# A hand-written order for three engines in blocks 2 to 8 of an FNet and MLP kernel

## The chip, the cores and the metric

The kernel runs on one core of one Trainium2 chip. Its metric is the device time of one execution in microseconds. A core has TensorE for matrix products, ScalarE and VectorE for elementwise work, GpSimd (POOL in the profile) and SyncE (SP), which here issues loads. Each engine works through its own list of instructions in a fixed order; where an instruction needs another engine's result, it waits at its place, and all behind it on that engine wait too.

## The reference

`x` has 2048 rows of 576 numbers. Its rows are normalized, and two branches are added to it: a Fourier mixing and an MLP.

```
xn = (x - mean(x)) / sqrt(var(x) + 1e-5)                      # over the 576
a, b = xn @ dft_hid_re.T, xn @ dft_hid_im.T                   # 576 x 576
y = dft_seq_re @ a - dft_seq_im @ b                           # 2048 x 2048
out = x + y + relu(xn @ w1) @ w2                              # w1 576 x 4608, w2 4608 x 576
```

All inputs are float32. The kernel splits each operand of a product into a high and a low half in float16 and adds three products of halves.

## The kernel before

**The MLP.** The 4608 hidden columns are cut into nine blocks of 512 (`b`, 0 to 8), the 2048 rows into four groups of 512 (`g`, 0 to 3). One pair (b, g) is a step; step n = 4b + g. In blocks 2 to 8, steps 8 to 35, both products of a step are done by a scheme of Strassen and Winograd with seven products of half size.

`step_products(n)` gives the first layer of a step: products P1, P5, P6, P2, P7, P3, P4 (`product`, line 579), which accumulate in four banks of PSUM: `u`, `v` and `w`, the last one of two in turn. P1 leaves a sum in `u`, P6 and P7 add to it, and so on, so each bank has to be read at the right time: `c11`, `c22`, `r21` and `s4` are copies by ScalarE; the adds to `c11` (from `v`), `c22` (from `u`) and `r21` (from `w`) are VectorE's. From these come the operands of the second layer in float16, a high part by ScalarE and a low part by VectorE: for A11, A22 and A12 (`value`, `last`) and for the sums S1 to S4 (`end_hi`, `end_lo`, two halves each). `rests` (line 598) are eight small matmuls for the last 64 rows of the inner dimension, of this step's P3 and P4 and of the next step's P2 and P5.

`mlp2(b, g, n)` (line 685) is product n = 0 to 6 of the second layer, called m0 to m6 below: 12 matmuls into one of two accumulators of two banks each, and then its drain. For n = 0, 2, 3, 6 ScalarE copies the bank with a scale (line 710), for n = 1, 4, 5 VectorE adds it (line 714). After n = 1, 4, 5, 6 GpSimd issues a transfer that adds the result to a buffer in DRAM (`spill`, line 717). m0, m2, m4 and m6 go into one accumulator one after another, m3 and m5 into another, so the drain of one stands before the next. The second layer runs one step behind the first: within step n the m's are those of step n - 1.

**The order in a step** is the tuple at lines 1197 to 1204. It is the order in which the program names its instructions:

```
(run, P1), (left, 0), (run, P5), (end, 0), (end, 0), (m, 0), (brief, 1), (left, 1),
(run, P6), (end, 0), (end, 0), (run, P2), (t_sum, 0), (m, 1), (used, P2), (more, 0), (ready, 1),
(run, P7), (t_sum, 0), (ready, 1), (m, 2), (used, P7), (count, 0), (m, 3), (brief, 1),
(rest, 0), (run, P3), (brief, 1), (m, 4), (used, P3), (t_sum, 0), (ready, 1),
(run, P4), (used, P4), (t_sum, 0), (m, 5), (ready, 1), (count, 0),
(m, 6), (brief, 3),
```

The framework's planner makes each engine's list from it. It takes the named order as a priority and lets a later instruction go ahead where it reckons that an earlier one isn't ready. `tc.issue_after(i)` makes an instruction stand behind instruction i on its engine; `behind(key)` (line 243) does so with an instruction kept in `order`.

**Preparing the next block.** In the four steps of block b the weights of block b + 1 are loaded and made ready. `prepare_block` (line 876) lists this as 39 small steps in `todo`; `work()` (line 1037) takes the next one, and `brief` and `ready` in the tuple call it ten times in a step. In that list: loads of two halves of W1 (`load_w1`, SyncE); their largest magnitudes (`max_w1`, VectorE), a reduction over the partitions on GpSimd, a power of two from it (`power`, tiny instructions on VectorE); the split into halves (`split_w1b`, ScalarE and then VectorE, line 229 and 230); the sums of quarters that the scheme needs (`sums_w1`, lines 774 to 778); the same for W2 (`sum_w2` on ScalarE, `split_w2`, `sums_w2`). In block 8 the list has the hidden DFT matrix instead (`power_d`, `prepare_d`, `load_d`; line 1092 and 1096).

**Counts.** Beside that, the magnitudes of the sequence DFT matrices are summed, 64 blocks of 512 KB, one after another through one buffer. `part(k)` (line 1153) takes the block that has been loaded (`sum_c`, line 1145, ScalarE) and starts the load of the next (line 1138, SyncE). Six parts of the hidden DFT matrix (`first_d` and `max_d`, a maximum on VectorE) stand in the same list at places 24 to 29. A step calls `count` twice, and `more` a third time where g is odd. Three parts are taken before step 8, ten in each later block.

**After the steps** comes the product with the hidden DFT matrix (line 1324), whose first pass also has the second layer of the last step, in an order that is already fixed for TensorE, ScalarE and VectorE by `pinned` (line 1442); then the product with the sequence DFT matrices (line 1570).

Of the kernel before, what the change touches and what calls it, by code (L numbers as in the profile page):

```python
# [26 lines left out]
NQ = NF // 2  # L27
# [27 lines left out]
def kernel(  # L55
# [496 lines left out]
    banks1, ends, gates = [], [], {}  # L552
# [6 lines left out]
    def step_products(n):  # L559
# [57 lines left out]
        def value(q, src):  # L617
            hi, lo = h[:, 0, q], h[:, 1, q]
            nc.scalar.activation(hi, src, AF.Relu)  # L619
            stt(lo, src, 0.0, hi, ALU.max, ALU.subtract)  # L620

        def end_hi(i):
            with behind("free"):
                order["s"] = nc.scalar.activation(h[:, 0, S1 + 2 * i :][:, :2], stage[:, 1 + 2 * i :][:, :2], AF.Copy).ins  # L624
# [5 lines left out]
        def sums_h():  # L630
            nc.scalar.activation(r21, r21, AF.Relu)
            stt(s3, c11, 0.0, r21, ALU.max, ALU.subtract)
            stt(s1, c22, 0.0, r21, ALU.max, ALU.add)
            stt(s2, c22, 0.0, s3, ALU.max, ALU.subtract)

        def last():
            hi, lo = h[:, 0, A12], h[:, 1, A12]
            nc.scalar.activation(hi, s4, AF.Copy)
            tt(lo, s4, hi, ALU.subtract)
            tt(s4, s4, s2, ALU.subtract)  # L640
            for i in range(NQ):
                ends.extend((lambda i=i: end_hi(i), lambda i=i: end_lo(i)))

        free = {
            P1: lambda: freed(nc.scalar.activation(c11, u, AF.Copy)),
            P2: lambda: freed(tt(c11, v, c11, ALU.add), "vfree"),
            P6: lambda: freed(nc.scalar.activation(r21, u, AF.Copy)),  # L647
            P5: lambda: freed(nc.scalar.activation(c22, w, AF.Copy)),
            P7: lambda: freed(tt(c22, u, c22, ALU.add), "vfree"),  # L649
            P3: lambda: freed(tt(r21, w, r21, ALU.add), "vfree"),  # L650
            P4: lambda: freed(nc.scalar.activation(s4, u, AF.Relu)),
        }
        use = {
            P2: lambda: value(A11, c11),
            P7: lambda: value(A22, c22),
            P3: sums_h,
            P4: last,
        }
# [26 lines left out]
    def mlp2(b, g, n):  # L685

# [8 lines left out]
        for c in range(2):  # L695
            for i in range(NQ):
                h, w = hs[b, g, i], w2s[b, i]
                for j, (x, y) in enumerate(((0, 0), (0, 1), (1, 0))):
# [4 lines left out]
                    ).ins  # L703
        if n in (0, 2, 3, 6):
# [325 lines left out]

    steps = [(b, g) for b in range(NB) for g in range(NG)]
# [89 lines left out]

    NP = NT // 2
# [28 lines left out]
    parts[24:24] = [(first_d, max_d, m) for m in range(ND)]  # L1151
# [13 lines left out]
    for n in range(2, len(steps)):  # L1165
        b, g = steps[n]
        pb, pg = steps[n - 1]
        if g == 0 and b:
            if b + 1 < NB:
                todo += prepare_block(b + 1)  # L1170
            else:
                d = power_d()
                todo += [lambda: (load_d(0), next(d)), lambda: None, lambda: later(d)]
                todo += prepare_d(0) + [lambda: load_d(1)] + [lambda: None] * 3 + prepare_d(1)[:DA]
# [10 lines left out]
        if b >= BB:  # L1185
            run, rests = step_products(n)
            used = lambda q: run(q, True)
            m = lambda q: mlp2(pb, pg, q)
            end = lambda q: ends and ends.pop(0)()
            ready = lambda q: [work() for _ in range(q)]  # L1190
            brief = lambda q: [work(True) for _ in range(q)]
            count = lambda q: passes and passes.pop(0)()
            left = lambda q: n == 2 * NG and lates[-1][q]()
# [74 lines left out]
    while todo:  # L1268
        work()
# [371 lines left out]
```

## Time and profile before

| | |
|---|---|
| median of 3 runs | 1233.02 us (1230.89 to 1233.25) |
| profiled execution | 1233.9 us, span 1232.1 us |
| granted clock of TensorE, mean over the span | 0.999 |
| steps 8 to 35 | from 194 to 792 us of the span |
| busy: TensorE, VectorE, ScalarE, GpSimd | 98%, 81%, 57%, 15% |

How to read it. A row of instruction groups has the line, the engine, the operation, what it writes and reads, the number of instructions, then busy time and the mean of one, and then the idle time of the engine before them with what ended it. PE is TensorE, PEld its loading of weights, DVE is VectorE, ACT is ScalarE. In a timeline the first two columns are the start and the duration in us; a part in brackets is idle time of that engine just before and what ended it. In the chain of work that ended last, the columns are start, duration and what. A row of waits has the total, the number and the longest.

Matmuls overlap: 26 matmuls of the steps start within 2.84 us, though each is listed with 0.27 us. So the busy share of TensorE says little, and the spacing of its starts is what counts. Some records of matmuls are missing from a trace.

### The profile page before, as it was taken

The page shows a single profiled execution, that of the slowest core. Times are in us where ns is not written, and L with a number is a line of the kernel's source. Part 1 is how long each engine was busy: PE and PEld are TensorE (multiplying, and loading weights), DVE is VectorE, ACT ScalarE, POOL GpSimd, SP SyncE. Part 2 cuts the span into 40 slices and gives each one's busy share as a digit, 9 for nine tenths or more (in the row PEclk, how much of TensorE's full clock was granted, in tenths as well). Part 3 has the DMA queues.
Part 4 walks back from the last instruction along what each step waited for, and adds up shares of the span by engine and source line. Part 5 has one row for each costly group of instructions (what it writes and reads, how often), then busy time and mean ns, then how long its engine had stood idle before and what let it go on. Part 6 is the DMA issues. An engine that isn't in the chain of part 4 may idle for free.

```text
span 1232.1 us, 24558 instructions
## 1 busy us (share of the span) xinstructions
PE 1211.8 (98%) x10173; PEld 957.2 (78%) x10173; DVE 999.3 (81%) x1629; ACT 707.8 (57%) x1073; POOL 189.6 (15%) x229
## 2 busy tenths in 40 slices
PE   8999999999999999999999999999999999999998
PEld 7665557888888788888888877877777777777776
DVE  8998899778887887778877877567898878787875
ACT  5756456776675576767767766555654333333332
POOL 2431211112121111112121211234300000000000
PEclk9999999999999999999999999999999999999999
DMA  8994545767566666667576666620165244433320
GB/s 314 209 155 106 76 74 139 149 143 156 125 155 141 144 152 162 138 161 155 132 157 142 147 151 149 106 35 1 62 194 162 94 155 161 153 122 131 128 88 20
DMA packets 84063, 164.64 MB, mean 134 GB/s; under 512 B 22640, under 2 KB 43632, under 8 KB 83952
## 3 DMA queue, kind: packets, MB, share of 16 engines
q1 hardware_dynamic: 61168, 120.61, 30.8%
q0 software_dynamic: 22784, 42.48, 24.0%
q8 instruction: 79, 1.29, 0.4%
q14 instruction: 32, 0.26, 0.1%
HBM read 110.76 MB, written 53.08 MB: 133 GB/s over the span
## 4 chain that ended last, share of the span: by engine, by line
PE 66%; DVE 18%; issue 7%; ACT 4%; DMA 4%; POOL 1%; SPq 0%; ACTq 0%; POOLq 0%; DVEq 0%
PE p L1570 24%; PE p L699 19%; PE bank L593 16%; DVE arena L230 3%; PE U L1324 3%; PE W L1324 2%; DMA arena<-in_w_dram 1%; PE p L392 1%; DVE arena L714 1%; DMA spill<-arena 1%; DVE arena L468 1%; ACT arena L229 1%; PE bank L612 1%; DVE c_mf L161 1%; DVE arena L628 1%
## 5 line engine op out<-in xcount | busy, mean ns | idle before, releaser
L699 PE MATMUL p<-arena 128*128 128x288 f16 x3024 | 400.5, 286 | 8.4 <-DVE arena L714 6.6
L699 PEld LDWEIGHTS <-arena 128*128 128x128 f16 x3024 | 295.7, 98 | 86.3 <-issue 10.3
L1570 PE MATMUL p<-arena 128*128 128x288 f16 x2688 | 329.9, 286 | 0.4 <-DVE arena L1576 0.4
L1570 PEld LDWEIGHTS <-arena 128*128 128x128 f16 x2688 | 263.0, 98 | 67.1 <-issue 0.7
L593 PE MATMUL bank<-arena 128*128 128x256 f16 x2580 | 304.8, 273 | 1.3 <-ACT arena L647 0.9
L593 PEld LDWEIGHTS <-arena 128*128 128x128 f16 x2580 | 250.1, 98 | 39.3 <-issue 7.7
L229 ACT ACTIVATE arena<-arena,sc_c 128x1024 f16<-128x1024 f32 x112 | 124.3, 1144 | 194.3 <-DVE arena L1422 69.7
L717 POOL DMA_DIRECT2D spill<-arena x144 | 128.6, 914 | 568.3 <-DVE arena L714 520.4
L230 DVE SCALAR_TENSOR_TENSOR arena<-arena,sc_c 128x1024 f16<-128x1024 f32 x112 | 140.9, 1281 | 47.7 <-ACT arena L229 47.7
L710 ACT ACTIVATE arena<-p,c_ub 128x576 f32<-128x576 f32 x144 | 105.5, 734 | 44.2 <-PE p L699 40.6
L230 DVE SCALAR_TENSOR_TENSOR arena<-arena,c_sw 128x640 f16<-128x640 f32 (+2 forms) x118 | 98.2, 847 | 20.2 <-ACT arena L229 19.8
L229 ACT ACTIVATE arena<-arena,c_sw 128x640 f16<-128x640 f32 (+3 forms) x118 | 90.1, 795 | 23.4 <-DVE c_sw L171 12.2
L628 DVE TENSOR_TENSOR arena<-arena 128x1024 f16<-128x1024 f32 x56 | 68.5, 1223 | 42.3 <-ACT arena L624 42.1
L392 PE MATMUL p<-arena 128*128 128x128 f16 (+1 forms) x680 | 100.0, 304 | 1.2 <-ACT arena L347 1.1
L714 DVE SCALAR_TENSOR_TENSOR arena<-p,c_ub,arena 128x576 f32<-128x576 f32 x108 | 87.4, 810 | 8.4 <-PE p L699 5.6
L1324 PEld LDWEIGHTS <-arena 128*128 128x128 f16 x738 | 71.6, 98 | 19.7 <-issue 1.9
L392 PEld LDWEIGHTS <-arena 128*128 128x128 f16 x680 | 53.9, 100 | 39.6 <-issue 3.8
L619 ACT ACTIVATE arena<-arena 128x512 f16<-128x512 f32 x56 | 35.2, 628 | 66.4 <-DVE arena L649 37.9
L1145 ACT ACTIVATE arena<-arena 128x1024 f32<-128x1024 f32 x64 | 67.0, 1048 | 6.4 <-DMA arena<-in_cim_dram 3.4
L1576 DVE SCALAR_TENSOR_TENSOR arena<-p,us_c,arena 128x288 f32<-128x288 f32 x112 | 57.5, 513 | 13.8 <-PE p L1570 13.4
L624 ACT ACTIVATE arena<-arena 128x1024 f16<-128x1024 f32 x56 | 58.8, 1050 | 0.0
L1324 PE MATMUL U<-arena 128*128 128x288 f16 x400 | 55.8, 286 | 0.0
(151 smaller groups left out, 1098.6 us busy)
## 6 DMA issues: line engine op xcount, KB each, us to landing
spill<-arena POOLq DMA_DIRECT2D x144, 288.0 KB, 4.8
arena<-in_cre_dram SPq DMA_DIRECT2D x64, 512.0 KB, 4.0
arena<-in_cim_dram SPq DMA_DIRECT2D x64, 512.0 KB, 4.8
arena<-in_w_dram SPq DMA_DIRECT2D x17, 640.0 KB, 5.9
arena<-in_w_dram SPq DMA_DIRECT2D x18, 576.0 KB, 4.7
arena<-spill SPq DMA_DIRECT2D x40, 144.0 KB, 2.2
arena<-in_x_dram SPq DMA_DIRECT2D x16, 288.0 KB, 7.1
spill<-in_x_dram SPq DMA_DIRECT2D x16, 288.0 KB, 6.2
```

The costliest lines, as they stand in the source:

```text
L229: nc.scalar.activation(hi, src, AF.Copy, scale=s).ins,
L230: nc.vector.scalar_tensor_tensor(lo, src, s, hi, ALU.mult, ALU.subtract).ins,
L392: order["m1"] = nc.tensor.matmul(ps[:, cols], w1s[b, i // 2][:, hl, i % 2 * KT + k], xT[g][:, kx, cols], start=(start and n == 0), stop=(s ...
L593: nc.tensor.matmul(ps[:, i], l, r, start=first and i == m == 0, stop=m == len(todo) - 1, skip_group_check=not first or i > 0,)
L628: order["lo"] = nc.vector.tensor_tensor(lo, stage[:, 1 + 2 * i :][:, :2], hi, ALU.subtract).ins
L699: order["pe"] = nc.tensor.matmul(ps[:, c], h[:, x, qa, c * P : (c + 1) * P], w[:, y, qb], start=first and i == 0 and j == 0, stop=i == NQ ...
L710: freed(nc.scalar.activation(o, ps, AF.Copy, scale=us[b]))
L714: add = nc.vector.scalar_tensor_tensor(o, ps, us[b], o, ALU.mult, ALU.add)
L717: nc.gpsimd.dma_start(spill[g, row, col], o, accum_op=ALU.add)
L1145: nc.scalar.activation(f, f, AF.Abs, scale=2.0**-10, accum_out=sums_c[:, n, q : q + 1])
L1324: nc.tensor.matmul(ps, l, r, start=first and m == 0, stop=m == len(todo) - 1, skip_group_check=not first,)
L1570: nc.tensor.matmul(ps, w[:, a, k], r[:, c, RQ[rq]], start=first and k == 0 and j == 0, stop=k == HK - 1 and j == 2, skip_group_check=not f ...
```

## The change

From step 8 on every piece of work in a step goes through `pinned`, which has moved up in the file: it makes each instruction that a piece puts on TensorE, ScalarE or VectorE stand behind the last instruction that an earlier piece put on that engine. The planner then has nothing to choose on these three engines. SyncE and GpSimd aren't pinned.

The order of TensorE's products in the tuple stays P1, P5, m0, P6, P2, m1, P7, m2, m3, `rests`, P3, m4, P4, m5, m6. The copies, adds, high and low parts are now named one by one. `mlp2` is cut into its matmuls (`mlp2_mm`) and its drain with the spill (`mlp2_out`); the drain of m6, `s42` (the last of the sums), `lo0`, `hi1` and `lo1` are done in the next step, as `pend`.

The preparation of the next block no longer comes from a list that is worked off; `chores_w(b)`, or `chores_d()` in block 8, gives each piece a step g and a slot, a to g, of the tuple. What is left of the preparation of this block's W2, three splits, stands in slot b of step g = 0, with the loads of the next W1 behind it.

`max_d` goes from places 24 to 29 of the counts to places 11, 21, 31, 41, 51 and 61, one in each block from 2 to 7. The counts of a step stand behind P2, behind the drain of m3 where g is odd, and behind `hi0`.

```diff
-        def run(q, used=False):
-            if used:
-                return use[q]()
-            product(q)
-            if q in free:
-                free[q]()
-
-        return run, rests
+        ops = {q: (lambda q=q: product(q)) for q in (P1, P2, P3, P4, P5, P6, P7)}
+        ops.update({
+            "c11": copy(c11, u), "v": add(c11, v), "r21": copy(r21, u), "c22": copy(c22, w),
+            "u": add(c22, u), "w": add(r21, w), "s4": copy(s4, u, AF.Relu),
+            "hi11": hi(A11, c11), "lo11": lo(A11, c11), "hi22": hi(A22, c22), "lo22": lo(A22, c22),
+            "relu": lambda: nc.scalar.activation(r21, r21, AF.Relu),
+            "s3": lambda: stt(s3, c11, 0.0, r21, ALU.max, ALU.subtract),
+            "s1": lambda: stt(s1, c22, 0.0, r21, ALU.max, ALU.add),
+            "s2": lambda: stt(s2, c22, 0.0, s3, ALU.max, ALU.subtract),
+            "hi12": hi(A12, s4, AF.Copy),
+            "lo12": lambda: tt(h[:, 1, A12], s4, h[:, 0, A12], ALU.subtract),
+            "s42": lambda: tt(s4, s4, s2, ALU.subtract),
+        })
...
+    def pinned(f, *a):
+        traced = nc.cur_bb.bb.instructions
+        n = len(traced)
+        with ExitStack() as s:
+            for i in tails.values():
+                s.enter_context(tc.issue_after(i))
+            f(*a)
+        for i in traced[n:]:
+            if i.engine in ENGINES:
+                tails[i.engine] = i
...
+    def chores_w(b):
+        c, n = {}, b + 1
+        c[0, "b"] = todo[:] or [lambda i=i, k=k: split_w2(b, i, k) for i, k in ((0, 2), (1, 1), (1, 2))]
+        del todo[:]
+        c[0, "b"] += [lambda i=i: load_w1(n, i) for i in range(NQ)]
+        for i in range(NQ):
+            p = power_w1(n, i)
+            c[i, "e"] = [lambda i=i: max_w1(n, 2 * i)]
+            c[i, "f"] = [lambda i=i, p=p: (max_w1(n, 2 * i + 1), next(p))]
+            c[i + 1, "a"] = [lambda p=p: next(p, None)]
+            c[i + 1, "b"] = [lambda i=i, k=k: split_w1b(n, i, k) for k in (0, 1)]
+            c[i + 1, "c"] = [lambda i=i: sums_w1(n, i)]
+            c[i + 1, "d"] = [lambda i=i, k=k: split_w1b(n, i, k) for k in (2, 3)] + [lambda i=i: load_w2(n, i)]
+        p2 = power_w2(n)
+        c[2, "e"] = [lambda: sum_w2(n, 0)]
+        c[2, "g"] = [lambda: (sum_w2(n, 1), next(p2))]
+        c[3, "a"] = [lambda: next(p2, None)]
+        c[3, "b"] = [lambda: split_w2(n, 0, 0)]
+        c[3, "c"] = [lambda: sums_w2(n, 0)]
+        c[3, "d"] = [lambda: split_w2(n, 1, 0)]
+        c[3, "e"] = [lambda: sums_w2(n, 1)]
+        c[3, "f"] = [lambda: split_w2(n, 0, 1)]
+        return c
+
+    def chores_d():
+        c, d = {}, power_d()
+        c[0, "b"] = [lambda i=i, k=k: split_w2(NB - 1, i, k) for i, k in ((0, 2), (1, 1), (1, 2))] + [lambda: load_d(0)]
+        c[0, "e"] = [lambda: next(d)]
+        c[1, "a"] = [lambda: next(d, None)]
+        e0, e1 = prepare_d(0), prepare_d(1)
+        for k, q in zip("bcdef", (e0[:2], e0[2:4], e0[4:6], e0[6:7], e0[7:8])):
+            c[1, k] = q
+        c[2, "b"] = e0[8:] + [lambda: load_d(1)]
+        c[2, "f"] = e1[:1]
+        for k, q in zip("bcd", (e1[1:3], e1[3:4], e1[4:5])):
+            c[3, k] = q
+        return c
...
-    parts[24:24] = [(first_d, max_d, m) for m in range(ND)]
+    for m in range(ND):
+        parts.insert(11 + 10 * m, (first_d, max_d, m))
...
+            if n == BB * NG:
+                pend = {"lo0": lates[-1][0], "hi1": lates[-1][1]}
+            ops, rests = step_products(n)
+            now = lambda k: pinned(ops[k])
+            then = lambda k: pinned(pend.pop(k)) if k in pend else None
+            m = lambda q: pinned(mlp2_mm, pb, pg, q)
+            out2 = lambda q: pinned(mlp2_out, pb, pg, q)
+            slot = lambda k: [pinned(f) for f in chores.pop((g, k), ())]
...
-                (run, P1), (left, 0), (run, P5), (end, 0), (end, 0), (m, 0), (brief, 1), (left, 1),
...
-                (m, 6), (brief, 3),
+                (now, P1), (then, "out6"), (then, "s42"), (now, "c11"), (slot, "a"), (then, "lo0"),
+                (now, P5), (slot, "b"), (now, "c22"), (then, "hi1"),
+                (m, 0), (slot, "c"), (out2, 0), (now, P6), (now, "r21"), (slot, "d"),
+                (now, P2), (count, 0), (now, "v"), (now, "hi11"), (m, 1), (out2, 1),
+                (now, P7), (now, "u"), (now, "lo11"), (now, "hi22"), (m, 2), (out2, 2), (then, "lo1"), (slot, "e"),
+                (m, 3), (out2, 3), (slot, "f"), (more, 0), (t_sum, 0), (rest, 0), (now, P3), (now, "w"), (now, "relu"), (t_sum, 0), (now, "lo22"),
+                (slot, "g"), (m, 4), (out2, 4), (now, "s3"), (now, "s1"), (now, "s2"),
+                (now, P4), (now, "s4"), (now, "hi12"), (now, "hi0"), (t_sum, 0), (count, 0), (m, 5), (out2, 5), (now, "lo12"),
+                (t_sum, 0), (m, 6),
             ):
                 do(q)
+            pend = {k: ops[k] for k in ("s42", "hi1", "lo0", "lo1")}
+            pend["out6"] = lambda b=pb, g=pg: mlp2_out(b, g, 6)
...
-                (P1, 0), ("end", 0), ("end", 0), ("c11", 0), ("mlp", 0), ("end", 0), ("end", 0),
+                (P1, 0), ("pend", "out6"), ("pend", "s42"), ("c11", 0), ("pend", "hi1"), ("pend", "lo0"),
+                 ("mlp", 0), ("pend", "lo1"),
```

More of the change, by code (lines that the diff above doesn't have):

```diff
@@ L1167 @@
         pb, pg = steps[n - 1]
[L1168 to L1174, printed above, removed]
+        if g == 0 and 0 < b < BB:
+            todo += prepare_block(b + 1)
+        if g == 0 and b >= BB:
+            chores = chores_w(b) if b + 1 < NB else chores_d()
         if b == 0 and g + 1 < NG:
@@ L1185 @@
         if b >= BB:
[L1186 to L1193, printed above, removed]
-            t_sum = lambda q: next(tq, None)
+            if n == BB * NG:
+                pend = {"lo0": lates[-1][0], "hi1": lates[-1][1]}
@@ L1197 @@
+            rest = lambda q: pinned(rests, n + 1 if n + 1 < len(steps) else None)
             for do, q in (
[L1198 to L1201 removed]
```

79 lines of the change are left out of this document (25 added, 54 removed).

## The prediction

> **What bounds the kernel now.** I read the page first, for the engines' shares, then the chain of work that ended last, then the timeline of TensorE, then the waits of TensorE alone from 188 to 800 us, where the steps lie that the change touches.
>
> ```profile
> span 1232.1 us, 24558 instructions
> PE 1211.8 (98%) x10173; PEld 957.2 (78%) x10173; DVE 999.3 (81%) x1629; ACT 707.8 (57%) x1073; POOL 189.6 (15%) x229
> ...
> 210.22 1.64 PE bank L593 x14
> 231.21 1.63 PE bank L593 x14
> ...
> 784.17 1.63 PE bank L593 x14
> ```
>
> The last three rows, of the chain, are the start of product P3 in the first, the second and the last of the 28 steps. A step without a stall lasts 231.21 - 210.22 = 20.99 us (its neighbours give 20.98). From the first P3 to the last are 27 steps: 784.17 - 210.22 = 573.95 us, where 27 x 20.98 would be 566.46. So only 7.5 us of stall lie in 27 steps. The first step is counted apart, with the calendar of a quiet step (timeline of TensorE):
>
> ```profile
> 194.17 3.22 PE L593 MATMUL bank<-arena 128*128 128x256 f16 x28
> ...
> 210.16 1.70 PE L593 MATMUL bank<-arena 128*128 128x256 f16 x14
> ...
> 217.63 3.00 PE L593 MATMUL bank<-arena 128*128 128x256 f16 x26
> 220.47 1.63 PE L699 MATMUL p<-arena 128*128 128x288 f16 x12
> 221.94 3.00 PE L593 MATMUL bank<-arena 128*128 128x256 f16 x26
> 224.78 1.63 PE L699 MATMUL p<-arena 128*128 128x288 f16 x12
> 226.25 1.47 PE L593 MATMUL bank<-arena 128*128 128x256 f16 x12
> 227.56 3.10 PE L699 MATMUL p<-arena 128*128 128x288 f16 x24
> 230.60 0.61 PE L612 MATMUL bank<-arena 64*128 64x256 f16 x8
> 231.14 1.70 PE L593 MATMUL bank<-arena 128*128 128x256 f16 x14
> 232.68 1.63 PE L699 MATMUL p<-arena 128*128 128x288 f16 x12
> ```
>
> From P1 to P3 the first step takes 210.16 - 194.17 = 15.99 us, the quiet one 231.14 - 217.63 = 13.51. The first has four matmuls more (28 and 28 for 26 and 26), at (220.47 - 217.63) / 26 = 0.109 us each, so it loses 2.04. Ceiling of any gain in the steps: 7.5 + 2.0 = 9.5 us, 0.8%. Who holds TensorE:
>
> ```profile
> PE p L699 <- DVE arena L714: 3.9, 5, 2.1
> PE bank L612 <- DVE arena L649: 1.2, 1, 1.2
> PE bank L593 <- ACT arena L647: 0.9, 1, 0.9
> PE p L699 <- DVE arena L628: 0.6, 1, 0.6
> PE bank L593 <- ACT arena L645: 0.2, 1, 0.2
> ...
> 417.63 1.47 PE L593 MATMUL bank<-arena 128*128 128x256 f16 x12 [0.94 <-ACT arena L647]
> ...
> 739.51 1.63 PE L699 MATMUL p<-arena 128*128 128x288 f16 x12 [2.09 <-DVE arena L714]
> ...
> 734.01 0.82 DVE L230 SCALAR_TENSOR_TENSOR arena<-arena,c_sd 128x576 f16<-128x576 f32 x1 [3.68 <-DMA spill<-arena]
> ...
> L161 DVE TENSOR_REDUCE max_d<-arena x6: 1144/1145/1153, 397.6 to 441.5; 128x1 f32<-128x960 f32 x6
> ```
>
> These waits add to 6.8 us; the rest of the 9.5 hides under the modelled ends of the matmuls before. Most wait for VectorE, which drains a bank (L714) or frees one (L649) too late. Two places explain themselves: six `max_d` of 1.145 us each fall into block 4 (397.6 to 441.5), and in block 8 a split stands in VectorE's queue for 3.68 us, until the spill of an old buffer has landed, before the drain that TensorE needs.
>
> **The change part by part.** *TensorE.* Its order P1, P5, m0, P6, P2, m1, P7, m2, m3, rests, P3, m4, P4, m5, m6 is the one that the rows show; pinning it is worth nothing, and no matmul goes. The work of ScalarE, VectorE and the queues is the same but for places. So the change is worth the stalls it takes away less those it makes.
>
> *The steady step.* I lay the new order of the fullest kind (g = 1: two scale steps, both splits, sums, three counts) against the calendar, P1 at 0: m0 2.84, P6 4.31, m1 7.15, P7 8.62, m2 9.93, m3 11.40, rests 12.97, P3 13.51, m4 15.05, P4 16.52, m5 18.05, m6 19.52, next step 20.99. Durations:
>
> ```profile
> L628 DVE TENSOR_TENSOR arena<-arena 128x1024 f16<-128x1024 f32 x56 | 68.5, 1223 | 42.3 <-ACT arena L624 42.1
> L714 DVE SCALAR_TENSOR_TENSOR arena<-p,c_ub,arena 128x576 f32<-128x576 f32 x108 | 87.4, 810 | 8.4 <-PE p L699 5.6
> 232.88 0.69 DVE L650 TENSOR_TENSOR arena<-bank,arena 128x512 f32<-128x512 f32 x1 [0.39 <-PE bank L593]
> L230 DVE SCALAR_TENSOR_TENSOR arena<-arena,c_sw 128x640 f16<-128x640 f32 (+2 forms) x118 | 98.2, 847 | 20.2 <-ACT arena L229 19.8
> L624 ACT ACTIVATE arena<-arena 128x1024 f16<-128x1024 f32 x56 | 58.8, 1050 | 0.0
> L710 ACT ACTIVATE arena<-p,c_ub 128x576 f32<-128x576 f32 x144 | 105.5, 734 | 44.2 <-PE p L699 40.6
> L619 ACT ACTIVATE arena<-arena 128x512 f16<-128x512 f32 x56 | 35.2, 628 | 66.4 <-DVE arena L649 37.9
> 230.77 1.04 ACT L1145 ACTIVATE arena<-arena 128x1024 f32<-128x1024 f32 x1
> 231.71 0.19 ACT L1145 ACTIVATION_READ_ACCUMULATOR arena<-arena 128x1 f32 x1
> ```
>
> A bank is readable 0.2 us after its product (232.88 against 231.14 + 14 x 0.109). ScalarE: the drain of m6 before to 0.9, `c11` 1.5 to 2.1, two splits to 3.3, `c22` 3.8, `hi1` 4.8, drain of m0 5.4, `r21` 5.8 to 6.4 (P7 asks at 8.62), two splits to 7.8, a count to 8.85. VectorE: `s42`, scales and `lo0` to 2.4, splits to 4.3, five sums to 6.3, splits 7.2 to 8.8, `v` 8.7 to 9.4 although P2 was readable at 7.35, drain of m1 to 10.1 (m3 asks at 11.40: slack 1.3, the least), `u` 10.1 to 10.8 (rests 12.97), `lo11`, `lo1` to 12.6 (m4 15.05), two maxima to 14.3, `w` 15.2 to 15.9, drain of m4 17.5 (m6 19.52), `s3`, `s1`, `s2` to 19.6, drain of m5 20.5 (next m0 23.8), `lo12` 21.1. ScalarE again: `s4` 18.2 to 18.8 (next P1 20.99), `hi0` to 20.7, last count to 21.8, drain of m6 1.5 into the next step, `c11` 2.1 (P6 4.31). No product waits: stall 0. With g = 3 the last count may be a `max_d`; it then ends by 21.3 and the drain of m5 by 22.0, against 23.8: 0, not two blocks' worth as now. The first step no longer has `sums_x` ahead of `u`: its 2.0 go, since `u` ends 2.1 before rests asks.
>
> *Queues moved past.* On GpSimd the spill of m6 goes out where its drain ends, as now; `hi`, `lo` and the leftover splits stand behind the drain of m6, m0 or a count on ScalarE. On SyncE the load of the next W1 now waits for three splits: out at 3.7 and 5.2; `max_w1` asks at 12.6, 8.9 us after the first, and the longest landing below is 9.0 with a median of 4.7, so it is worth nothing here.
>
> *Block 8.* The drain of m6 that now runs a step later writes to the new buffers, so the last spill out of the old ones is that of m5; the split that waited stands in slot e, at about 14, eight us after that spill can land (4.8 us, below). So 3.2 of the 9.5 go here. In its place slots a to d of g = 1 are heavier: four splits and five sums of 0.75, so `v` comes at 9.5 to 10.8 and the drain of m1 up to 0.8 behind m3. I take 0.5, between 0 and 0.8.
>
> ```profile
> 726.17 0.75 DVE L1102 TENSOR_TENSOR arena<-arena 128x576 f32<-128x576 f32 x1
> ```
>
> *Waits of the counts.* A count holds all of ScalarE until its block of the DFT matrix has landed, and the planner can no longer let others pass. The one buffer makes it a round trip: count, load, count. The rows: what the counts waited for their loads (6.4 us, 7 times); then issue to landing of all such loads, of the one beside a W2 load at 238 us, of one alone at 530 us, and of the spills.
>
> ```profile
>   ACT arena L1145: 6.4, 7
> ...
> DMA to landing us min/median/max: 3.1/4.7/9.0
> ...
> DMA to landing us min/median/max: 8.6/8.6/8.6
> ...
> DMA to landing us min/median/max: 3.1/3.1/3.1
> ...
> spill<-arena POOLq DMA_DIRECT2D x144, 288.0 KB, 4.8
> ```
>
> In an odd step three counts follow: 8.85 + L1 + 1.14 + L2 + 1.14, then the drain of m6 and `c11`, 1.3, must end by 25.3 (next P6): L1 + L2 at most 12.9. From about 11 on, late splits already push the drain of m1 past m3, by up to 0.9. Two medians are 9.4: 0. Two maxima are 18: 5.1 + 0.9 = 6.0 per block, 42 us in seven. In g = 1 the load of W2 leaves 0.4 us ahead of the first, so I estimate L1 6.5 and L2 4, 10.5 in all: nearest the medians, and I take 0.5 us for all blocks. The Trainium skill, "DMA: Bandwidth & Descriptors", "Issuing engines are not separate DMA queues", says that transfers from all queues run on the same 16 engines and interleave; the trace agrees (8.6 us beside another load, 3.1 alone). Read strictly, L1 would be 8.6, with L2 4.7 in all 13.3: 0.4 + 0.9 = 1.3 per block and some 9 us in all, which gives 1233.
>
> *Sum.* The profiled execution took 1233.9 us (span 1232.1), 0.9 above the median 1233.0. 1233.9 - 9.5 + 0.5 + 0.5 = 1225.4; against the median **1224.5 us**. The DFT stage behind gets five of the moved operations, as before, and nothing else.
>
> **The rivals.** *Late loads* (slower). The count after m3 of a g = 1 step waits, ScalarE stands, and P6 and m3 of the next step pay. It decides from a stall of 1.4 us per block on (9.5 / 7), L1 + L2 about 13.4. At 16 it is 3.1 + 0.9 = 4 per block, 28 in all: 1224.5 + 28 = 1252; just above the point 1236 to 1240. For it: 8.6 at 238 us, and an order that can't give way. Against it: that load had both spills of a step's end beside it, and in the new place only that of m1; the counts stand 6 us apart or more.
>
> *Part of the gain.* VectorE's queue stays too full in block 8 and where `max_d` meets a step of g = 3 (by the adding-up above its queue then ends 1 us after the step does): the 3.9 us that TensorE waited for L714 stay, 1224.5 + 3.9 = 1228.4. For it: the least slack is 1.3 us. Against it: every drain stands in the new order where its product ends, ahead of the chores that follow.
>
> *The pins do little.* The planner's order was near this one (27 steps with 7.5 us of stall); new waits at other places equal the old ones: 1231 to 1235.
>
> **How the numbers follow.** About 0.2%, 2.5 us, is what a measurement of this kernel tells from no change. Forecast (1222 to 1227) 0.55; part of the gain 0.13; the pins do little, or late loads that just cancel, 0.08; late loads beyond that 0.18. The case that just cancels is the one that the Trainium skill's page "DMA: Bandwidth & Descriptors" speaks for. There is also another wait of the fixed order that I don't see, such as a drain behind a split: 0.06, at about 1240. Faster 0.68, same 0.08, slower 0.24. The floor is 1233.0 - 9.5 = 1223.5, less the scatter of the runs (1230.89 to 1233.25, so 2 us): 1221.5. The top, 1240, leaves out the worse half of the late loads, 0.1, and half of the unseen, 0.03. The forecast's own range is 1222 to 1227.
>
> **What would show it.** Right: P3 to P3 20.98 us in every step, 566 to 568 us over 27; the waits of TensorE between 188 and 800 us under 1.5 us; no wait of 3.68 us for a spill in block 8; `max_d` spread from 270 to 700 us. Late loads: ScalarE's waits for the DFT matrix, 6.4 us before (row above), well above 20, and TensorE waiting for `c11` and the drain of m1. Wrong at the root: the same stalls at block 4 or 8 in spite of the order, or steps that are all longer by the same amount.

## The result, and the profile after

The changed kernel takes 1225.98 us (1223.57 to 1226.38), the kernel before 1233.02 (1230.87 to 1234.75): a ratio of 0.9942, with a 95% interval of 0.9925 to 0.996. The change saves about 7 us, 0.6%. Its profiled execution took 1225.98 us, with a span of 1223.9; before it was 1233.9 and 1232.1, so the two traces differ by 8.2 us of span.

The page after, first the engines' shares, then the shares of the chain that ended last:

```profile
span 1223.9 us, 24586 instructions
PE 1209.4 (99%) x10173; PEld 956.5 (78%) x10173; DVE 1003.6 (82%) x1629; ACT 713.8 (58%) x1073; POOL 192.2 (16%) x229
...
PE 80%; DVE 13%; ACT 3%; issue 2%; DMA 2%; SPq 0%; ACTq 0%; DVEq 0%
```

The work is the same; TensorE's share of the chain goes from 66% to 80%. The waits of TensorE from 188 to 800 us, and then its timeline:

```profile
PE bank L593 <- ACT arena L618: 0.9, 1, 0.9
PE p L688 <- DVE arena L707: 0.2, 1, 0.2
```

```profile
209.01 1.70 PE L593 MATMUL bank<-arena 128*128 128x256 f16 x14
...
731.81 1.63 PE L688 MATMUL p<-arena 128*128 128x288 f16 x12 [0.16 <-DVE arena L707]
...
775.66 1.70 PE L593 MATMUL bank<-arena 128*128 128x256 f16 x14
```

Five rows of waits with 6.8 us in all have become two with 1.1. From the first P3 to the last pass 775.66 - 209.01 = 566.65 us, 0.2 above the 566.46 of 27 quiet steps; before, it was 573.95. Added up from the spacing of the matmuls' starts, the stalls of steps 8 to 35 are 9.6 us before and 1.4 after. The difference, 8.2, is that of the spans: from the last P3 to the end of the span 448 us pass in both. Two stalls are left. One is 0.33 us, at m3 in block 8 (the row at 731.81). The other, 1.05 us, stands in the first step. In the rows of ScalarE and TensorE there:

```profile
200.08 1.06 ACT L464 ACTIVATE arena<-arena 128x1024 f16<-128x1024 f32 x1 [2.27 <-DVE arena L458]
201.05 1.42 ACT L229 ACTIVATE arena<-arena,c_sw 128x576 f16<-128x576 f32 x2
...
202.38 0.57 ACT L618 ACTIVATE arena<-bank 128x512 f32<-128x512 f32 x1
202.86 0.73 ACT L703 ACTIVATE arena<-p,c_ub 128x576 f32<-128x576 f32 x1
203.48 0.59 ACT L618 ACTIVATE arena<-bank 128x512 f32<-128x512 f32 x1
...
204.12 1.47 PE L593 MATMUL bank<-arena 128*128 128x256 f16 x12 [0.89 <-ACT arena L618]
```

P7 waits for the last copy, `r21` at 203.48. ScalarE does `c22`, the drain of m0 and `r21` without a pause; they are late because the two leftover splits (L229) stand ahead of them, and these came late because ScalarE waited 2.27 us for work that VectorE still had from the step before.

The tightest place of a g = 1 step, in step 9 and in block 8 (timeline, the splits of ScalarE and then VectorE):

```profile
223.85 1.44 ACT L229 ACTIVATE arena<-arena,c_sw 128x640 f16<-128x640 f32 x2 [0.34 <-DVE arena L770]
...
224.71 1.55 DVE L230 SCALAR_TENSOR_TENSOR arena<-arena,c_sw 128x640 f16<-128x640 f32 x2 [0.90 <-ACT arena L229]
226.17 0.68 DVE L621 TENSOR_TENSOR arena<-bank,arena 128x512 f32<-128x512 f32 x1
226.77 0.81 DVE L707 SCALAR_TENSOR_TENSOR arena<-p,c_ub,arena 128x576 f32<-128x576 f32 x1
...
730.34 0.68 DVE L621 TENSOR_TENSOR arena<-bank,arena 128x512 f32<-128x512 f32 x1
730.94 0.81 DVE L707 SCALAR_TENSOR_TENSOR arena<-p,c_ub,arena 128x576 f32<-128x576 f32 x1
```

In step 9 P1 starts at 216.49. The second pair of splits waits 0.90 us for ScalarE, so the drain of m1 ends 11.1 us after P1, where m3 asks at 11.4: the slack is 0.3 us.

The counts, on ScalarE in the same step, then its waits for their loads:

```profile
232.59 1.06 ACT L1192 ACTIVATE arena<-arena 128x1024 f32<-128x1024 f32 x1 [2.25 <-DMA arena<-in_cim_dram]
...
238.45 1.06 ACT L1192 ACTIVATE arena<-arena 128x1024 f32<-128x1024 f32 x1 [1.17 <-DMA arena<-in_cim_dram]
```

```profile
ACT arena L1192 <- DMA arena<-in_cim_dram: 5.6, 6, 2.3
ACT arena L1192 <- DMA arena<-in_cre_dram: 0.7, 2, 0.4
```

The two loads were issued at 226.66 and 233.77 and had landed at 232.57 and 238.43: 5.9 + 4.7 = 10.6 us, the most of any g = 1 step. In all ScalarE waits 6.3 us for its counts' loads, 6.4 before. Neither of TensorE's two stalls stands behind such a wait.

### The profile page after: what moved, and what is told of

The parts are those of the page before. It is cut to its first block, busy times and chain, and to the rows that moved or that the text cites. A ratio compares the mean times of both kernels' runs of the same rounds, so it can differ in the third digit from the quotient of the medians.

```text
span 1223.9 us, 24586 instructions
## 1 busy us (share of the span) xinstructions
PE 1209.4 (99%) x10173; PEld 956.5 (78%) x10173; DVE 1003.6 (82%) x1629; ACT 713.8 (58%) x1073; POOL 192.2 (16%) x229
## 3 DMA queue, kind: packets, MB, share of 16 engines
q8 instruction: 79, 1.29, 0.4%
## 4 chain that ended last, share of the span: by engine, by line
PE 80%; DVE 13%; ACT 3%; issue 2%; DMA 2%; SPq 0%; ACTq 0%; DVEq 0%
PE p L688 26%; PE p L1606 24%; PE bank L593 22%; PE U L1373 3%; DVE arena L230 3%; PE W L1373 2%; DMA arena<-in_w_dram 1%; PE p L392 1%; PE bank L612 1%; DVE arena L468 1%; ACT arena L229 1%; DVE arena L707 1%; DVE arena L1424 1%; PE V L1373 1%; DVE arena L451 1%
## 5 line engine op out<-in xcount | busy, mean ns | idle before, releaser
L229 ACT ACTIVATE arena<-arena,sc_c 128x1024 f16<-128x1024 f32 x112 | 124.3, 1144 | 194.3 <-DVE arena L1471 69.9
L621 DVE TENSOR_TENSOR arena<-bank,arena 128x512 f32<-128x512 f32 x84 | 57.8, 688 | 51.7 <-PE bank L593 50.7
L229 ACT ACTIVATE arena<-arena,c_sw 128x640 f16<-128x640 f32 (+3 forms) x118 | 89.1, 794 | 17.0 <-DVE c_sw L803 6.9
L618 ACT ACTIVATE arena<-bank 128x512 f32<-128x512 f32 x112 | 66.4, 593 | 49.3 <-PE bank L593 49.2
L624 ACT ACTIVATE arena<-arena 128x512 f16<-128x512 f32 x84 | 52.9, 630 | 52.7 <-DVE arena L621 51.8
```

The source lines that it names most:

```text
L229: nc.scalar.activation(hi, src, AF.Copy, scale=s).ins,
```

## The experiments

The profile says that the stalls went. It does not say which part of the change took them away: other places for `max_d` and the chores, the new order of names, or the pins. In the table "27 steps" is the time from the first P3 to the last less 566.46, and "stalls" the sum by spacing over steps 8 to 35.

| kernel | median us | ratio to before (95%) | 27 steps | stalls |
|---|---|---|---|---|
| before | 1233.02 | | 7.5 | 9.6 |
| changed | 1225.98 | 0.9942 (0.9925 to 0.996) | 0.2 | 1.4 |
| E1 changed, not pinned | 1234.2 | 1.0011 (0.9998 to 1.0023) | 8.2 | 10.5 |
| E2 before, `max_d` spread | 1233.09 | 0.9997 (0.9986 to 1.0009) | 6.0 | 8.1 |
| E3 changed, `max_d` together | 1225.8 (one time) | | 1.0 | 2.1 |
| E4 before, late split last | 1233.49 | 0.9997 (0.9986 to 1.0009) | 7.1 | 9.3 |
| E5 before, E2 and E4 | 1232.93 | 0.9999 (0.9988 to 1.001) | 4.5 | 6.5 |
| E6a changed, loads twice | 1336.01 (one time) | | 109.8 | |
| E6b changed, loads once and a half | 1310.6 (one time) | | 84.6 | |
| E7 changed, two places eased | 1224.34 | 0.9933 (0.9917 to 0.995) | -0.1 | 0.8 |
| E8 pins on VectorE alone | 1227.63 | 0.9953 (0.9938 to 0.9968) | 2.8 | 4.0 |
| E9 pins on ScalarE alone | 1226.06 | 0.9943 (0.9928 to 0.9958) | 0.5 | 2.8 |
| E10 before, its own order pinned | 1255.4 | 1.0178 (1.0161 to 1.0195) | 27.2 | 29.3 |
| E11 changed, first step eased otherwise | 1226.02 | 0.9946 (0.993 to 0.9963) | 2.2 | 2.3 |

**E2, E4, E5: the two places, each mended in the kernel before.** E2 spreads `max_d` as the change does. E4 puts the split that waited for the spill at the end of its list. E5 does both.

```diff
# E2
-    parts[24:24] = [(first_d, max_d, m) for m in range(ND)]
+    for m in range(ND):
+        parts.insert(11 + 10 * m, (first_d, max_d, m))
# E4
-            + pieces((7, 9, 1), (15, 7, 2), (8, 0, 3), (11, 3, 2), (13, 5, 2))
+            + pieces((7, 9, 1), (8, 0, 3), (11, 3, 2), (13, 5, 2), (15, 7, 2))
```

> The kernel before with one part of the change alone: the six max_d stand at places 11, 21, 31, 41, 51 and 61 of the counts, not at 24 to 29. My theory (two crowded places of VectorE held TensorE) expects the stalls of block 4, 3.0 us in the trace before, to go and no wait of TensorE between 365 and 455 us; about 1230 us, 2.5 to 3 us under before. The rival (the planner's order is what costs, wherever the maxima stand) expects the stalls to move to the blocks that get a max_d: within 1 us of before.

> The kernel before with the five last pieces of the hidden DFT matrix in another order, so that the two that overwrite the old sum buffers come last, 4 to 6 us later. My theory expects no wait of 3.68 us for a spill on VectorE in block 8, and the 3.2 us of stall near 735 to 741 us gone: about 1230 us. The rival (VectorE is too full there anyway) expects a stall of 1 us or more at m3 of the same step, and less than 2 us of gain.

> The kernel before with both small edits, max_d spread and the two pieces last, and no pin and no named order. If the two crowded places carry the gain, the stalls are 9.5 - 3.0 - 3.2 = 3.3 us and the time about 1227, 6 us under before and within 2 us of the changed kernel. If the pinned order carries it, less than 3 us is gained.

None of the three differs from the kernel before. In E2 stalls in and behind block 4 are still there, at 417.6, 426.4 and 448.1 us (0.66, 0.68 and 0.67 by spacing), 2.1 us where it was 3.0, though the nearest `max_d` are at 368.4 and 455.4. Nor did the stalls move to the blocks that got a `max_d`, as the rival had it: in those the only new one over 0.2 us has 0.24. The rows of E2 at the first of the three:

```profile
415.49 0.43 DVE L776 TENSOR_TENSOR arena<-arena 128x256 f32<-128x256 f32 x1
415.83 1.22 DVE L628 TENSOR_TENSOR arena<-arena 128x1024 f16<-128x1024 f32 x1
...
416.96 0.68 DVE L646 TENSOR_TENSOR arena<-bank,arena 128x512 f32<-128x512 f32 x1
417.56 0.81 DVE L714 SCALAR_TENSOR_TENSOR arena<-p,c_ub,arena 128x576 f32<-128x576 f32 x1
...
418.43 1.63 PE L699 MATMUL p<-arena 128*128 128x288 f16 x12 [0.49 <-DVE arena L714]
```

Sums of the preparation (L774 to L776) and a low part (L628) stand ahead of the add `v` and the drain that m3 needs. None of these waits at that point; they only stand ahead. In the kernel before, block 4 also has a chore that itself waits: in its g = 2 step a split stands on ScalarE until its scale (L171, VectorE) is there, with the copy `c22` behind it:

```profile
413.70 0.83 ACT L229 ACTIVATE arena<-arena,c_sw 128x640 f16<-128x640 f32 x1 [3.68 <-DVE c_sw L171]
```

One `max_d` (411.57 to 412.72) stands on VectorE ahead of that scale. In E2 it doesn't, and the same split still waits 1.95 us. So `max_d` lengthened a wait that was there without it.

In E4 the stall at 735 to 741 us goes, and with it the wait for the spill. But the step behind it loses 2.3 us, where it lost 0.6 before. The largest part, 1.4 us by spacing, is P6 waiting for `c11`. The rows of ScalarE, and the last one of TensorE:

```profile
742.17 1.06 ACT L1145 ACTIVATE arena<-arena 128x1024 f32<-128x1024 f32 x1 [2.77 <-DMA arena<-in_cre_dram]
...
748.09 1.06 ACT L1145 ACTIVATE arena<-arena 128x1024 f32<-128x1024 f32 x1 [3.13 <-DMA arena<-in_cre_dram]
...
753.15 2.02 PE L593 MATMUL bank<-arena 128*128 128x256 f16 x17 [1.24 <-ACT arena L645]
```

Two counts hold ScalarE until their loads have landed. The first stands ahead of `relu`, behind which come a sum and then the drain that m6 waits for; the second stands ahead of three splits and `c11`. In the kernel before, the second count waits 1.73 us and the first not at all. So the split on the spill did cause the stall at its place; with it gone, other late chores took over a part.

E4 is not clean: `prepare_d` is used for the second half of the matrix too, and behind the steps E4 and E5 take 450.1 us, 2 more than before. So of the 3 us that E5's steps gained by the column of 27 steps, 2 were given back in the next stage by the edit itself. A version that reorders the first half alone was not tried. What holds without it: E2's gain of 1.5 us in the steps is too small to be seen in the time, and E5 leaves 6.5 of 9.6 us.

**E1: the new order without pins.** All names stand in the new order, in the new places, but the planner is free again.

```diff
-            now = lambda k: pinned(ops[k])
-            then = lambda k: pinned(pend.pop(k)) if k in pend else None
-            m = lambda q: pinned(mlp2_mm, pb, pg, q)
+            now = lambda k: ops[k]()
+            then = lambda k: pend.pop(k)() if k in pend else None
+            m = lambda q: mlp2_mm(pb, pg, q)
...
```

> The changed kernel without the pins in the steps: same named order, same fixed places of the preparation, same spread, but the planner may again let later instructions of ScalarE and VectorE go first. If the places carry the gain, the stalls stay at 1 to 3 us and the time at 1225 to 1228. If the pins carry it, several us of stall come back, 1230 or more.

E1 also lacks one constraint of the kernel before, by which the high parts of the sums (`end_hi`) stood behind a copy or drain of ScalarE; that was not tried alone. TensorE's products stand in the same order in the kernel before, the changed one and E1. The whole gain is gone: 10.5 us of stall, nearly all for drains on VectorE. The first row of TensorE's waits:

```profile
PE p L688 <- DVE arena L707: 7.4, 10, 1.1
```

One of the ten, m6 of step 10 in the timeline of all engines:

```profile
254.71 1.16 ACT L780 ACTIVATE arena<-arena 128x1152 f16<-128x1152 f32 x1
...
256.13 0.37 POOL L167 PARTITION_ALL_REDUCE top<-c_mw  x1 [4.49 <-ACT arena L780]
256.53 0.17 DVE L170 TENSOR_SCALAR half<-top 128x2 f32<-128x2 f32 x1 [3.40 <-POOL top L167]
...
257.08 0.68 DVE L621 TENSOR_TENSOR arena<-bank,arena 128x512 f32<-128x512 f32 x1
...
257.80 0.63 ACT L641 ACTIVATE arena<-arena 128x512 f32<-128x512 f32 x1 [1.84 <-DVE arena L621]
...
259.07 0.81 DVE L707 SCALAR_TENSOR_TENSOR arena<-p,c_ub,arena 128x576 f32<-128x576 f32 x1
...
259.94 1.63 PE L688 MATMUL p<-arena 128*128 128x288 f16 x12 [1.12 <-DVE arena L707]
```

The planner let the scale of the next W2 (L170) go ahead of the add `w` (L621) on VectorE. That scale needs a reduction on GpSimd, which needs the sum of W2 on ScalarE (L780). VectorE stands 3.40 us, the last 2.1 of them with `w` readable behind it (P3 starts at 252.64; with 14 matmuls and the 0.2 us of the prediction that gives 254.4). `relu` waits for `w`, the sums for `relu`, the drain for the sums, and m6 for the drain. The same happens in the g = 2 step of every block from 2 to 7: six waits of 3.40 us and stalls of 1.29, 1.22, 0.93, 0.62, 1.29 and 0.65 us, 6.0 of the 10.5. In the kernel before, that scale never waits more than 0.7 us for GpSimd. So E1 does not bring the old stalls back; it has others of the same kind. In the changed kernel the order is the other way round:

```profile
252.71 0.69 DVE L621 TENSOR_TENSOR arena<-bank,arena 128x512 f32<-128x512 f32 x1 [1.82 <-PE bank L593]
...
254.26 0.82 DVE L707 SCALAR_TENSOR_TENSOR arena<-p,c_ub,arena 128x576 f32<-128x576 f32 x1 [0.26 <-PE p L688]
...
259.25 0.16 DVE L170 TENSOR_SCALAR half<-top 128x2 f32<-128x2 f32 x1
```

**E10: the old order with pins.** Every piece of a step of the kernel before goes through `pinned`, in the order in which its tuple names it.

```diff
-                do(q)
+                pinned(do, q)
...
-            ready = lambda q: [work() for _ in range(q)]
-            brief = lambda q: [work(True) for _ in range(q)]
+            ready = lambda q: [pinned(work) for _ in range(q)]
+            brief = lambda q: [pinned(work, True) for _ in range(q)]
```

> The kernel before with its own order and its list of small steps, each piece pinned on the three engines as it is named. If pins alone carry the gain, 1225 to 1228. If they need the new order too, in which a drain stands where its product ends and each chore has a place that its engine has room for, stalls of 4 us or more stay and the time is 1228 to 1236.

22 us slower than before, with about 1 us of stall a step on average (0 to 2.8). The first two rows of TensorE's waits (188 to 830 us), and one of those waits on VectorE:

```profile
PE p L699 <- DVE arena L714: 9.4, 9, 2.0
PE bank L612 <- DVE arena L649: 5.9, 9, 1.1
```

```profile
235.55 0.88 DVE L230 SCALAR_TENSOR_TENSOR arena<-arena,c_sw 128x640 f16<-128x640 f32 x1 [2.12 <-ACT arena L229]
236.35 0.81 DVE L714 SCALAR_TENSOR_TENSOR arena<-p,c_ub,arena 128x576 f32<-128x576 f32 x1
```

A split that waits 2.12 us for ScalarE stands ahead of the drain, and now nothing may pass it. So the pins alone harm, and the new order and places alone do nothing; the four cells are 1233.0 (old order, free), 1255.4 (old, pinned), 1234.2 (new, free) and 1226.0 (new, pinned). The order of the names and the places of the chores were not tried apart.

**E3: `max_d` put back together in the changed kernel** (E2's edit the other way round).

> The changed kernel with the six max_d back together at places 24 to 29, so that they fall into steps 1 to 3 of block 4, in the pinned order. My theory expects VectorE's queue to be late there: a max_d ahead of v holds the drain of m1 and the add u. In g = 1 the drain of m1 has a slack of 1.3 us and a max_d takes 1.145 plus what its load is late, so 1 to 5 us of stall in block 4 and 1227 to 1231 us. The rival (the pinned order has room enough for them) expects under 0.5 us of stall in block 4 and 1225 to 1226.

It adds 0.8 us of stall, 0.16 at 416.1 and 0.60 at 437.2, both in block 4. That is less than the theory's 1 us and more than the rival's 0.5; the one time, 1225.8, is the rival's. The six `max_d` cost 0.8 where the order is good; they were not what made most of the stalls before.

**E8, E9: pins on one engine alone.** `pinned` keeps the last instruction of VectorE alone (E8) or ScalarE alone (E9); the DFT stage keeps its pins on all three.

```diff
# E8; E9 has mybir.EngineType.Activation
-    tails = {}
+    tails, pins = {}, [mybir.EngineType.DVE]
...
-            if i.engine in ENGINES:
+            if i.engine in pins:
...
+    pins[:] = ENGINES
     for f in passes:
         f()
```

> The changed kernel with pins on VectorE alone in the steps. Without any pin, ten waits of TensorE for the drain of VectorE came back (7.4 us), because the planner put other work of VectorE ahead of that drain. The new theory (VectorE's order carries the gain) expects the changed kernel's time, 1225 to 1227, and under 2 us of stall. The rival (the two engines wait for each other, so both orders are needed) expects 1229 or more.

> The changed kernel with pins on ScalarE alone in the steps. The new theory expects the drains of VectorE to be late as without any pin: 6 to 10 us of stall and 1231 to 1235. If ScalarE's order is the one that counts, 1225 to 1227.

By then my theory was that VectorE's order carries the gain, as nearly all waits were for VectorE. It fell: E8 gains 5.9 us and keeps 4.0 of stall, short of its forecast, and E9, with VectorE left to the planner, gives all of the gain that can be measured, where the theory expected next to nothing. The intervals of E8, E9 and the changed kernel overlap, so the times don't rank the three. E9 at the place of E1's example:

```profile
254.23 0.69 DVE L621 TENSOR_TENSOR arena<-bank,arena 128x512 f32<-128x512 f32 x1 [1.31 <-PE bank L593]
...
254.95 0.63 ACT L641 ACTIVATE arena<-arena 128x512 f32<-128x512 f32 x1 [0.36 <-DVE arena L621]
...
255.66 1.16 ACT L780 ACTIVATE arena<-arena 128x1152 f16<-128x1152 f32 x1
...
256.23 0.81 DVE L707 SCALAR_TENSOR_TENSOR arena<-p,c_ub,arena 128x576 f32<-128x576 f32 x1
...
258.15 0.19 DVE L170 TENSOR_SCALAR half<-top 128x2 f32<-128x2 f32 x1
```

The pin holds the sum of W2 (L780) behind `relu` (L641) on ScalarE. `relu` needs the add `w`, and the scale needs the sum; so on VectorE the scale cannot stand ahead of `w` any more. The order of one engine reaches the other through the data. E9 has only four stalls, all in the first two steps. E8 has four, all in block 2. One is the changed kernel's own at P7; in the largest, 1.44 us, ScalarE, left free, makes P6 wait for its copy `c11`; the other two wait for the drain of m1, which stands behind splits that wait 0.90 us for ScalarE.

**E6a, E6b: later loads for the counts.** Each block of the sequence matrix is loaded twice (E6a), or its first half is loaded once more ahead of it (E6b). The computation is unchanged.

```diff
# E6a
             nc.sync.dma_start(f, blocks_c(n)[q])
+            nc.sync.dma_start(f, blocks_c(n)[q])
# E6b
+            nc.sync.dma_start(f[:, : HK // 2], blocks_c(n)[q][:, : HK // 2])
             nc.sync.dma_start(f, blocks_c(n)[q])
```

> The changed kernel with each counted block loaded twice, which adds about 3 us to each landing. The condition then expects the count behind P2 to be late too, and 5 to 6 us of stall at the end of each g = 1 step with 1 to 2 more at g = 3: 40 to 55 us in all, 1265 to 1280. ScalarE's waits for the DFT matrix rise from 6 us to over 60. If loads are hidden anyway, under 5 us.

> The changed kernel with half of each counted block loaded twice, 256 KB ahead of the whole 512 KB, which adds about 1.5 us to each landing. By the condition L1 + L2 at most 12.9 us, with 10.6 seen in g = 1, the sum is about 13.6: 0.7 us at P6 and 0.9 at m3 in each block, 10 to 14 us of stall in all, about 1237. If the counts have more room than the condition says, under 3 us.

Both missed their forecasts by far: 1336.01 where 1265 to 1280 was expected, and 1310.6 where about 1237 was. The edit is coarser than meant. The second load into the same buffer was issued only when the first had landed, so each pair is two round trips: 229.13 to 240.05 us for L1 and 241.30 to 249.22 for L2, 18.8 in all instead of 10.6. E6b's rows of that step:

```profile
240.13 1.06 ACT L1193 ACTIVATE arena<-arena 128x1024 f32<-128x1024 f32 x1 [8.72 <-DMA arena<-in_cim_dram]
...
242.33 5.56 PE L593 MATMUL bank<-arena 128*128 128x256 f16 x26 [4.12 <-ACT arena L618]
...
249.31 1.06 ACT L1193 ACTIVATE arena<-arena 128x1024 f32<-128x1024 f32 x1 [4.49 <-DMA arena<-in_cim_dram]
...
251.62 3.00 PE L593 MATMUL bank<-arena 128*128 128x256 f16 x26 [2.26 <-ACT arena L618]
```

This is the rival of late loads, made to happen: a count holds ScalarE, `s4` and `c11` come late, and P1 and P6 wait for them. From P3 to P3 this step took 31.0 us (230.57 to 261.57), 10.0 over a quiet one. The rival's formula, 5.9 over the condition and 0.9 for the drain of m1, gives 6.8. It left out the wait of P1 for `s4`, and the slower matmuls that followed (last section).

**E7, E11: the two stalls that are left.** Both move what stands in slots d, e and f of block 8's g = 1 step to e, f and g. In the first step E7 moves the leftover splits from slot b to d, E11 to e.

```diff
# E7
-        c[0, "b"] += [lambda i=i: load_w1(n, i) for i in range(NQ)]
+        if b == BB:
+            c[0, "d"] = c[0, "b"] + [lambda: load_w1(n, 1)]
+            c[0, "b"] = [lambda: load_w1(n, 0)]
+        else:
+            c[0, "b"] += [lambda i=i: load_w1(n, i) for i in range(NQ)]
...
-        for k, q in zip("bcdef", (e0[:2], e0[2:4], e0[4:6], e0[6:7], e0[7:8])):
+        for k, q in zip("bcefg", (e0[:2], e0[2:4], e0[4:6], e0[6:7], e0[7:8])):
# E11, beside this: the splits and the load to slot "e"
+        c[0, "e"] = first + c[0, "e"]
```

> The changed kernel with the two stalls that it has left taken out: in the first step the two leftover splits go behind r21, and in step g = 1 of block 8 the second half of the sums and what follows go behind lo1. The waits of TensorE between 188 and 800 us then go from 1.4 us to under 0.3, and the time to 1224.5, 1.4 us under the changed kernel. If something else stands right behind them, less than 0.7 us is gained.

> The changed kernel with the lighter block 8 of the run before, and in the first step the two leftover splits behind lo11 instead of ahead of v. There they held the drain of m1 and m3 lost 0.8 us; behind lo11 nothing of TensorE is due before the add w, which is late already. Expected: waits of TensorE between 188 and 800 us under 0.3 us, 0.6 us under the run before, 1223.5 to 1224.5. If the lateness only moves on to the drain of m4, m6 waits and nothing is gained.

E7 loses the stall of block 8, as forecast, and trades the 1.05 us of the first step for 0.81 at its m3, which waits for the drain of m1 (its row, in the timeline of TensorE):

```profile
205.70 1.63 PE L688 MATMUL p<-arena 128*128 128x288 f16 x12 [0.65 <-DVE arena L707]
```

It takes 1224.34 us, 0.9933 (0.9917 to 0.995): the best here, though the interval doesn't part it from the changed kernel's; that it stalls less, 0.8 us for 1.4, is what its trace shows. Its time is the forecast one, but its row of waits has 0.6 us, where under 0.3 was expected. E11 clears that place too, and stalls 1.75 us at m6 of the same step, as its expectation had allowed, and 0.55 in the next. In the first step both moves moved the stall on.

## Why the prediction was right, and where not

**Right, and for the reason given.** The ceiling of 9.5 us of stall in the steps (by spacing 9.6 before, 1.4 after; from the last P3 on both kernels take 448 us). The steady step of 20.98 us and 566.65 us over 27, within the forecast 566 to 568. TensorE's waits, 1.1 us against "under 1.5". Block 8: m3 waits for the drain of m1 by 0.33 us, where 0.5, between 0 and 0.8, stood in the sum; `v` starts there 730.34 - 720.09 = 10.25 us after P1, forecast 9.5 to 10.8 for it. No wait for a spill in block 8. The counts' loads: 10.6 us for L1 and L2 where 10.5 was estimated, and no stall from them (0.5 us was allowed). The strict reading of the Trainium skill's "DMA: Bandwidth & Descriptors", section "Issuing engines are not separate DMA queues", took 8.6 us for L1 beside the load of W2. The trace has 4.9 to 5.9 in the g = 1 steps of blocks 2 to 7, where a load of W2 goes out 0.4 us ahead; the load at the same place of the g = 3 steps, without one, takes 3.2 to 3.7. In one g = 2 step, also behind a load of W2, it took 8.4. So transfers do slow each other here, mostly by less than the strict reading.

**Wrong: the two places that explain themselves.** I put the stalls of block 4 (3.0 us by spacing) on the six `max_d` and 3.2 on one split in block 8, and so on two chores in wrong places. The profile showed these operations beside the stalls; that they alone caused them was my reading. Spread, `max_d` leaves 2.1 us of the stalls around block 4 (E2); put back together, they cost 0.8 (E3); the split moved, its stall goes, and late counts cost 1.7 us more in the next step (E4, with its flaw); both together leave 6.5 us (E5), where the explanation says 9.6 - 6.2 = 3.4. What the runs put in its place: the planner, left free, puts chores ahead of an add, a copy or a drain that TensorE needs, and often a chore that itself waits (E1's scale, E4's counts, the two splits before). That this is one cause for all the stalls before is read from the rows of a few of them; it was not tested stall by stall. The sum came out because it took all the stalls away wherever they came from, so this wrong step does not show in the number.

**Not told apart: the order and the pins.** The prediction put a worth on the pins for TensorE alone, nothing, and that was right: E1 has the list of TensorE that the changed kernel has. On ScalarE and VectorE it looked only at the new order as a whole. There the pins are worth 8 us with this order, and cost 22 with the old one. The rival "the pins do little", 1231 to 1235, did not come; among the runs its range fits E1, where the pins are missing.

**Mis-sized: the first step.** "Its 2.0 go" was wrong by half: 1.05 stays, but at P7 and for `r21`, not at `rests` for `u`. I had laid the g = 1 step against the calendar and taken the first for it, without the work that the step before leaves to both engines.

**Mis-sized: the least slack.** 1.3 us was forecast for the drain of m1 in a g = 1 step, and it is 0.3. The second pair of splits on ScalarE ended 223.85 + 1.44 - 216.49 = 8.8 us after P1, not 7.8, and VectorE's pair waits for it (0.90 us in the row at 224.71). The result was lucky here: a further 0.4 us would have made a stall in this step.

**Mis-sized: the late loads' price**, 4 us per block at L1 + L2 = 16. At 18.8 E6b lost 10 in the first such step and 84 in all. The mechanism was right, the path through P1 was missing, and the late loads don't happen in the changed kernel.

**Open.** Why the free planner's stalls lie mostly around block 4 and in block 8 before, and mostly at one place of every block from 2 to 7 in E1, was not found. Nor was E4's edit tried on the first half of the matrix alone.

## What to carry to other kernels

A wait that ends with an engine that is 82% busy is not yet a shortage of that engine: look at what stands ahead of the late instruction, and whether that was itself waiting. Pinning a list is worth as much as the list: before writing one, lay every engine's step against the bound engine's calendar, with each chore whose input comes late behind the drains that the bound engine needs. Ask, too, through which engine the chores' inputs come: here pins on that one alone (E9) measured as well as pins on all three. To test a suspected cause, take it away in the kernel before and put it back in the kernel after; here both runs spoke against `max_d`.

## What the runs showed of the hardware

In E6b TensorE's P1 waited 4.12 us for `s4`, and the 26 matmuls that followed started 0.213 us apart instead of 0.109 (5.56 us for a group that took 3.00 elsewhere): 2.7 us lost behind the wait itself. The window rows have the granted clock in the column behind POOL's:

```profile
238.00:248.00 10.00, 5.88 (x31) 3.98 (x30) 5.32 (x10) 3.84 (x6) 0.85 (x1) 0.66 0.60 144
248.00:262.00 14.00, 11.14 (x98) 8.79 (x96) 8.49 (x14) 10.97 (x18) 1.72 (x2) 1.00 0.65 149
```

Nine us later, after a wait of 2.26 us, 26 matmuls ran at full speed (the row at 251.62 above). The Trainium skill, "TensorE: Matmul & The Clock Gate", section "What's actually happening", says that the clock halves after an idle window of about 3.4 us and comes back after a busy one, and that the window doesn't start with the work. The half agrees. The length of the wait alone doesn't decide in this trace: at 293 us a wait of 2.20 us was followed by slow matmuls too, and the slow stretch at 242 us lasted 5.4 us. Over the steps of E6b all seven waits of more than 3.5 us were followed by ten or more slow matmuls, and of the seven between 2.0 and 2.6 us two were. For a rival that makes TensorE wait, this is a price on top: the mean clock of the span was 0.983 in E6b and 0.975 in E6a.

The doubled loads of E6b don't show what two transfers at once cost. In the trace the second load waits for the semaphore of the first: it was issued at 235.61, the first had landed at 235.59. So the program makes another round trip of it, 10.9 us for the pair where one load took 5.9.
